# A long convolution with soft mixture-of-experts slots: spectra and z stored from all 128 partitions in one transfer, with row orders to match

## The chip, the cores and the metric

The kernel runs on one core of a Trainium2 chip. The metric is the device time of one execution in microseconds (us), as the median of several runs. The span is the part of the profiled execution between its first and its last instruction.

## The reference

```python
def _attn_ref(x, h):                      # x (8, 5696, 128), h (5696, 128), float32
    L = 2 * S
    Yf = np.fft.rfft(x, n=L, axis=1) * np.fft.rfft(h, n=L, axis=0)[None]
    return np.fft.irfft(Yf, n=L, axis=1)[:, :S, :]

def _moe_ref(x, phi, w1, w2):             # x (45568, 128), 8 experts of 4 slots, F = 1024
    logits = x @ phi                      # (45568, 32)
    d = softmax(logits, over all tokens)  # with max subtracted
    slot_input = (d.T @ x).reshape(8, 4, 128)
    slot_out = [relu(slot_input[e] @ w1[e]) @ w2[e] for e in range(8)]
    c = softmax(logits, over slots)
    return c @ slot_out
```

The output of the convolution, flattened to 45568 rows, is the input of the second part.

## The kernel before

The convolution of length 5696 = 89 x 64 is a two-stage transform done with matmuls against tables. All data are float32. The work is one pass over nine sequences: h (g = 0), then the eight batches of x (g = 1 to 8). The order of everything is written out by hand as a list of words that `run` walks through (`low`, `high`, `fold`, `loadf`, `forward`, `backward`, `flush`, `loadz`, `loadr`, `product`, ...), each word calling one stage with a running number; the schedule is manual and every engine executes in that order.

- `load_x` (L183) loads eight columns of a sequence, near and mirrored ones, into `xc`, `fold` (L216) adds and subtracts them on POOL.
- `stage_a` (L229) is the first transform: matmuls at L240 into a PSUM bank, copied by ACT (L242) into a staging tile `fst`, and from there stored to DRAM. The 64 low rows of the spectrum go to `fl`, the high rows of two chunks together to `fh`. Even and odd partitions of `fst` hold the two halves of the mirrored columns.
- `load_g` (L262, issue at L273) loads a group of up to four spectrum rows as `gt`, with the 128 positions in the partitions. `stage_b1` multiplies by `wt` (L286, into `bt`), and for g > 0 DVE multiplies by the transform of h (L305, L312); `stage_b2` transforms back with `vt` (L327, into `bz`) and ACT copies the result into the one staging tile `zst` (L332). After each second group, rows of `z` are stored: `zm` for the first 64, `zr` for the other 26.
- `load_main` (L375) and `load_rest` (L386) load eight columns of all rows as `zc` and `zx`. `stage_c1` does the last transform: L413 with `zc` and the table `im`, then L418 with `zx` and `ir` into the same banks. The later stages (L431 to L564) turn, compute the logits, both softmaxes and the dispatch. After the last batch come the experts and the output.

Stores are not issued where they are made: they are put on the list `pending` as closures, and a word `flush` issues all of them from SP (their line in the profile is L224, in `flush`). SP issues all loads too, in the order of the words, and it waits in that order. In the program SP's transfers take eight completion semaphores in turn, so a transfer waits for the one eight places before it.

The stores of one staging tile are made in a loop over its halves, each from 64 partitions with a step of two:

```python
for a in range(2):
    dst = fh[g][a, j // 2] if high else fl[g][a, j]
    pending.append(partial(
        nc.sync.dma_start, out=dst.rearrange("n r x -> r n x"),
        in_=st[a::2, :, :, :].rearrange("r n c d -> r n (c d)")))
```

In DRAM `fl` has the dimensions half, chunk j, column n, row, so that the half is the slowest, and a load reads 128 rows that lie 32 KB apart (16 KB in `fh`). `zm` has (parity o, row, column), `zr` has (parity, part c, row, column). The tables `wq`, `im`, `ir` are permuted on the host to the order in which positions land in the partitions.

Of the kernel before, what the change touches and what calls it, by code (L numbers as in the profile page):

```python
# [19 lines left out]
def transform_tables(S, N1, N2, CH, LOW, MAIN):  # L20

    N, R1, HALF, P = N1 * N2, S // N2, N2 // 2, 2 * N2  # L30
    k1 = np.arange(N1)
    alpha = np.pi * (k1 + 0.5) / N1
    m1 = np.arange(R1) - (N1 - 1) / 2
    a1 = np.outer(m1, alpha)
    part = np.stack([np.cos(a1), -np.sin(a1), -np.cos(a1)], 1)
    s1 = np.zeros((P, 3, N2 + HALF))
    for p, r in ((slice(0, P, 2), slice(0, N2)), (slice(P - 4 * (R1 - N2) + 1, P, 4), slice(N2, R1))):
        s1[p, :, 0:LOW] = part[r, :, 0:LOW]
        s1[p, :, N2:N2 + N1 - LOW] = part[r, :, LOW:]
    a0 = np.outer(alpha, np.arange(N1 // 2) + 0.5)  # L40
    part = np.stack([np.cos(a0), -np.sin(a0), -np.cos(a0)], 1)
    NP = N1 // 2
    im = np.zeros((2, MAIN, 2, N2))
    ir = np.zeros((2, 2, HALF, N2))
    for o in range(2):
        for c in range(2):
            im[o, :, c, 0:NP] = part[0:MAIN, o + c]
            ir[o, c, 0:N1 - MAIN, 0:NP] = part[MAIN:, o + c]
    k2 = np.arange(N2)
    omega = np.pi * (k1[:, None] + 2 * N1 * k2[None] + 0.5) / N  # L50
    m2 = np.arange(HALF) - (N2 - 1) / 2
    a2 = m2[None, :, None] * omega[:, None, :]
    w = np.concatenate([np.cos(a2), np.sin(a2)], 1)
    back = np.arange(N2).reshape(2, HALF).T.reshape(-1)
    NU = (NP + 1) // 2
    turn = (N1 - 1) / 2 * alpha[:, None] + (N2 - 1) / 2 * omega
    wq = np.zeros((2, N2, NP, N2))
    vq = np.zeros((2, N2, NU, 2, N2))
    tn = np.zeros((2, N2, 2, (NU + 1) // 2, 2, 2))
    rows = np.arange(N2).reshape(2, HALF // CH, CH)  # L60
    near = rows.transpose(1, 2, 0).reshape(-1)
    far = rows.reshape(2, -1, 2, CH).transpose(1, 3, 2, 0).reshape(-1)
    for a in range(2):
        wq[a] = w[a::2].transpose(1, 0, 2)
        wq[a] = np.concatenate([wq[a][near, 0:LOW // 2], wq[a][far, LOW // 2:]], 1)
        for q in range(NP):
            vq[q % 2, :, q // 2, a] = w[2 * q + a][back].T
            tn[q % 2, :, 0, q // 4, a, q // 2 % 2] = np.cos(turn[2 * q + a]) / N
            tn[q % 2, :, 1, q // 4, a, q // 2 % 2] = np.sin(turn[2 * q + a]) / N
    im, ir, wq, vq, tn = [t.reshape(P, *t.shape[k:]) for t, k in  # L70
                          ((im, 2), (ir, 3), (wq, 2), (vq, 2), (tn, 2))]
    return [np.ascontiguousarray(t, dtype=np.float32) for t in (s1, im, ir, wq, vq, tn)]
# [3 lines left out]
def kernel(  # L76
# [47 lines left out]
        nc.inline_tensor(t, f"tab_{n}").ap()  # L124
        for n, t in zip(("s1", "im", "ir", "w", "v", "turn"),
                        transform_tables(S, N1, N2, CH, LOW, MAIN))]
    fl = [nc.dram_tensor(f"fl_{g}", (2, NJ, CH, 2 * LOW // 2, 2 * D), F32, kind="Internal").ap()
          for g in range(B + 1)]
    fh = [nc.dram_tensor(f"fh_{g}", (2, NJ // 2, CH, 2 * HALF, 2 * D), F32, kind="Internal").ap()
          for g in range(B + 1)]  # L130
    zm = [nc.dram_tensor(f"zm_{b}", (2, MAIN, HALF, 2, D), F32, kind="Internal").ap() for b in range(B)]
    zr = [nc.dram_tensor(f"zr_{b}", (2, 2, HALF, HALF, D), F32, kind="Internal").ap() for b in range(2)]
    cd = nc.dram_tensor("c_t", (P, B * NQ, Q, 2, MH), F32, kind="Internal").ap()

    const = ctx.enter_context(tc.tile_pool(name="const", bufs=1))
# [93 lines left out]
    def stage_a(c, high):  # L229

        g, j = divmod(c, NJ)
        st = apool.tile([P, CH, 2, D], F32, name="fst", tag="fst", bufs=4)
        if high:
            groups = [(c_, o, HALF, slice(HP, HP + HALF)) for c_ in (c - 1, c) for o in range(2)]
        else:
            groups = [(c, o, HALF, slice(r, r + HALF)) for o in range(2) for r in (0, HALF)]
        for q in range(2):
            p = bank()
            for i, (c_, o, m, cols) in enumerate(groups):
                nc.tensor.matmul(p[i * m:(i + 1) * m, :], s1[:, q + o, cols], columns(c_, o),  # L240
                                 start=True, stop=True)
            nc.scalar.activation(st[:, :, q, :],  # L242
                                 p[:, :].rearrange("p (n d) -> p n d", d=D), AF.Copy)
        for a in range(2):
            dst = fh[g][a, j // 2] if high else fl[g][a, j]
            pending.append(partial(
                nc.sync.dma_start, out=dst.rearrange("n r x -> r n x"),
                in_=st[a::2, :, :, :].rearrange("r n c d -> r n (c d)")))
        if high:
            for c_ in (c - 1, c):  # L250
                del folded[c_]
# [10 lines left out]
    def load_g(u):  # L262
        if u >= (B + 1) * NW:
            return
        g, w, us = parts(u)
        n = sum(k for _, k in us)
        t_ = bpool.tile([P, 4, 2, D], F32, name="gt", tag="gt", bufs=3)
        if 8 * w < LOW:
            src = fl[g].rearrange("a j n (o k) x -> (a j n o) (k x)", o=2)
        else:  # L270
            src = fh[g].rearrange("a j n (o k) x -> (a j n o) (k x)", o=4)
        k0 = 4 * w % (LOW // 2) * 2 * D
        nc.sync.dma_start(  # L273
            out=t_[:, 0:n, :, :].rearrange("p q c d -> p (q c d)"), in_=src[:, k0:k0 + n * 2 * D])
        gs[u] = t_

    def stage_b1(u):
# [38 lines left out]
    def stage_b2(u):  # L316
        g, w, us = parts(u)
        if g == 0:
            return
        m = len(us)  # L320
        y_ = prods.pop(u)
        bz = bps.tile([P, 2, 2, 2 * D], F32, name="bz", tag=("bt", "bz")[u % 2])
        for o, (i, n) in enumerate(us):
            for q in range(n):
                r = slice(q * HP, (q + 1) * HP)
                for a in range(2):
                    nc.tensor.matmul(bz[a * HP:(a + 1) * HP, q, o, :], vt[r, i, a, :],  # L327
                                     y_[r, a * m + o, :, :].rearrange("p c d -> p (c d)"),
                                     start=True, stop=True)
        n = us[0][1]  # L330
        e_ = w % 4
        nc.scalar.activation(zst[:, e_, 0:m, 0:n, :].rearrange("p o q x -> p q o x"),  # L332
                             bz[:, 0:n, 0:m, :], AF.Copy)
        if w % 2 == 0:
            return
        k = 4 * e_ + m * n
        sv = zst[:, :, :, :, :].rearrange("p u o q x -> p (u o q) x")
        q0 = 4 * e_ - 4
        k0 = 8 * (w - 1)
        for o in range(2):  # L340
            if k0 < MAIN:
                pending.append(partial(
                    nc.sync.dma_start,
                    out=zm[g - 1][o, k0:k0 + 16].rearrange("(q a) r c d -> (a r) q (c d)", a=2),
                    in_=sv[o::2, q0:k, :]))
                continue
            for c in range(2):
                pending.append(partial(
                    nc.sync.dma_start,
                    out=zr[g % 2][o, c, k0 - MAIN:k0 - MAIN + 2 * (k - q0)].rearrange("(q a) r d -> (a r) q d", a=2),  # L350
                    in_=sv[o::2, q0:k, c * D:(c + 1) * D]))

    zs, ys, Ls, ds = {}, {}, {}, {}
# [13 lines left out]
    def load_main(T):  # L367
        if T >= NT:
# [5 lines left out]
        n = 2 * CH  # L374
        nc.sync.dma_start(  # L375
            out=t_[0][:, :, :, :, :].rearrange("p h n c d -> p (h n c d)"),
            in_=zm[b].rearrange("o k r c d -> (o k) r (c d)")[:, j * n:(j + 1) * n].rearrange(
                "p r x -> p (r x)"))

    def load_rest(T):  # L380
        if T >= NT:
# [3 lines left out]
        n = 2 * CH  # L385
        nc.sync.dma_start(  # L386
            out=t_[1][:, :, :, :].rearrange("p h n d -> p (h n d)"),
            in_=zr[(b + 1) % 2].rearrange("o c k r d -> (o c k) r d")[:, j * n:(j + 1) * n].rearrange(
                "p r x -> p (r x)"))

    def load_pair(T):
        load_main(T)
# [2 lines left out]
    def stage_c1(T, between=lambda: None):  # L395
# [18 lines left out]
                                     zt[r, h_, :, c, :], start=True, stop=False)  # L414
        for h_ in range(2):
            for (o, c), p in ps.items():
                r = slice((2 * o + c) * HALF, (2 * o + c) * HALF + N1 - MAIN)
                nc.tensor.matmul(p[h_ * HP:(h_ + 1) * HP, :], ir[r, :], zx[r, h_, :, :],  # L418
                                 start=False, stop=True)
        ps = {k: p[:, :].rearrange("p (n d) -> p n d", d=D) for k, p in ps.items()}  # L420
# [196 lines left out]
    nc.scalar.dma_start(out=ir[:, :], in_=t_ir)  # L617
    for i in range(8):
        nc.scalar.dma_start(
            out=zr[i // 4][i // 2 % 2, i % 2, N1 - MAIN:].rearrange("k (j r) d -> (k j) (r d)", r=2 * CH),  # L620
            in_=zring[0][1][0:4 * (HALF - N1 + MAIN), :, :, :].rearrange("p h n d -> p (h n d)"))
    held = {}

# [304 lines left out]
```

## Time and profile before

| | |
|---|---|
| median of 3 runs | 813.05 us (812.43 to 819.96) |
| profiled execution, its own time | 815.48 us |
| its span | 813.7 us |
| mean granted TensorE clock | 0.949 |
| busy | PE 717.6 us (88%), DVE 629.5 (77%), ACT 429.3 (53%), POOL 411.5 (51%) |
| moved by DMA | 282.51 MB, 347 GB/s over the span |
| stores to `fl`, `fh` | 144 and 72 transfers of 256 KB |
| stores to `zm` | 64 of 512 KB |
| stores to `zr` | 32 of 256 KB and 32 of 160 KB |
| loads `gt`, `zc`, `zx` | 108 of mostly 512 KB, 32 of 1024 KB (two into the tile `zd`), 32 of 512 KB (two into `zy`) |

In the profile PE is TensorE, DVE is VectorE, ACT is ScalarE, POOL is GpSimd, SP is SyncE. A name with q (SPq) is the sequencer that issues transfers. L224 is line 224 of the kernel. `fl<-fst` is a transfer or instruction that writes `fl` and reads `fst`. A busy PE is not PE at its peak, since matmuls are pipelined and their ends are modelled.

### The profile page before, as it was taken

Reading aid. Unit: us, or ns where it says so; the run is one execution under the profiler, and the core shown is the slowest. Engines: PE = TensorE matmul, PEld = TensorE weight load, DVE = VectorE, ACT = ScalarE, POOL = GpSimd, SP = SyncE. Lnnn points to the kernel's source line nnn. Section 1 sums busy time; section 2 is a strip of 40 time slices with the busy share of each in tenths; the row PEclk is TensorE's granted clock in tenths of the full one; section 3 lists DMA queues with packets and bytes.
Section 4 is the critical chain, followed back from the end, with each engine's and each line's share of the span. In section 5 each row is a group of like instructions: output and inputs, shape, how many; then the busy total and the mean of one; then the engine's idle time right before and its main releaser. Section 6 shows DMA issues by size and latency. Waiting matters only on the chain.

```text
span 813.7 us, 22006 instructions
## 1 busy us (share of the span) xinstructions
PE 717.6 (88%) x8884; PEld 367.0 (45%) x8884; DVE 629.5 (77%) x895; ACT 429.3 (53%) x868; POOL 411.5 (51%) x368
## 2 busy tenths in 40 slices
PE   5767888869999999999999999999998887888893
PEld 1322233324544444444444455554444443356882
DVE  1029987638988998798999899988998997795642
ACT  2323345326666665566666666665664545474532
POOL 5655434224566666466656666655533443587000
PEclk9989999879999999999999999999999999999755
DMA  8999999999999999999999999999999898873998
GB/s 293 359 329 384 328 393 386 323 348 344 367 355 364 395 372 328 369 355 382 353 387 381 384 349 390 379 352 366 341 321 343 301 354 288 318 267 106 378 401 353
DMA packets 167661, 282.51 MB, mean 347 GB/s; under 512 B 11305, under 2 KB 130729, under 8 KB 162345
## 3 DMA queue, kind: packets, MB, share of 16 engines
q1 hardware_dynamic: 166552, 280.02, 96.6%
q8 instruction: 70, 1.15, 0.5%
q10 hardware_dynamic: 1008, 1.10, 0.4%
q14 instruction: 31, 0.25, 0.1%
HBM read 148.54 MB, written 132.53 MB: 345 GB/s over the span
## 4 chain that ended last, share of the span: by engine, by line
PE 55%; DMA 18%; DVE 15%; ACT 4%; POOL 2%; issue 2%; SPq 1%; ACTq 0%; DVEq 0%; POOLq 0%
PE bank L240 17%; PE bt L286 8%; PE bz L327 7%; PE bank L413 6%; DMA out_dram<-o 5%; PE bank L418 4%; DMA zx<-zr 4%; DVE yf L305 4%; DVE bt L305 4%; PE bank L441 3%; DMA xc<-in_h_dram 3%; PE bank L450 2%; DVE yf L312 2%; PE bank L540 2%; PE bank L564 2%
## 5 line engine op out<-in xcount | busy, mean ns | idle before, releaser
L240 PE MATMUL bank<-x,s 128*32 128x512 f32 x1728 | 209.1, 607 | 14.1 <-POOL x L216 8.3
L216 POOL TENSOR_TENSOR x<-xc 128x512 f32<-128x512 f32 x144 | 179.2, 1278 | 81.4 <-PE bank L240 55.5
L242 ACT ACTIVATE fst<-bank 128x512 f32<-128x512 f32 x216 | 125.8, 595 | 87.1 <-PE bank L240 50.7
L286 PE MATMUL bt<-gt,wt 64*64 64x256 f32 x1620 | 117.1, 398 | 27.4 <-DMA gt<-fl 9.4
L332 ACT ACTIVATE zst<-bz 128x1024 f32<-128x1024 f32 x96 | 93.0, 968 | 82.8 <-PE bz L327 72.5
L431 POOL TENSOR_TENSOR y<-y,op 128x512 f32<-128x512 f32 x64 | 78.4, 1225 | 112.8 <-DVE op L405 110.3
L305 DVE TENSOR_TENSOR yf<-bt,Hi 128x1024 f32<-128x1024 f32 x96 | 112.5, 1172 | 17.9 <-PE bt L286 17.8
L312 DVE TENSOR_TENSOR yf<-bt,yf 128x512 f32<-128x512 f32 x192 | 119.3, 663 | 3.3
L240 PEld LDWEIGHTS bank<-x,s 128*32 128x32 f32 x1728 | 56.1, 111 | 130.4 <-issue 90.8
L305 DVE TENSOR_TENSOR bt<-bt,Hr 128x1024 f32<-128x1024 f32 x96 | 113.0, 1177 | 0.0
L327 PE MATMUL bz<-yf,vt 64*64 64x256 f32 x1440 | 101.4, 390 | 4.8 <-DVE yf L312 4.4
L286 PEld LDWEIGHTS bt<-gt,wt 64*64 64x64 f32 x1620 | 54.7, 135 | 89.0 <-issue 28.8
L527 POOL TENSOR_TENSOR L<-L,rs 128x512 f32<-128x512 f32 x32 | 33.7, 1052 | 108.1 <-DVE rs L522 57.2
L327 PEld LDWEIGHTS bz<-yf,vt 64*64 64x64 f32 x1440 | 55.0, 137 | 41.1 <-DVE yf L312 12.9
L431 POOL TENSOR_TENSOR y<-y,om 128x512 f32<-128x512 f32 x54 | 64.3, 1190 | 2.1
L421 ACT ACTIVATE y<-bank 128x512 f32<-128x512 f32 x32 | 19.1, 597 | 87.4 <-PE bank L418 87.4
L441 PE MATMUL bank<-ident,y 109*128 109x109 f32 x512 | 59.2, 261 | 3.7 <-POOL y L431 1.7
L413 PE MATMUL bank<-zc,im 64*64 64x512 f32 x480 | 60.6, 599 | 0.1
L441 PEld LDWEIGHTS bank<-ident,y 109*128 109x128 f32 x512 | 49.7, 141 | 13.3 <-issue 7.4
L443 ACT ACTIVATE yt<-bank 128x360 f32<-128x360 f32 x128 | 52.6, 476 | 4.1 <-PE bank L441 3.9
L305 DVE TENSOR_TENSOR yf<-bt,turn 128x1024 f32<-128x1024 f32 (+1 forms) x12 | 14.1, 1171 | 52.3 <-PE bt L286 52.3
L405 DVE TENSOR_TENSOR y<-bank,y 128x512 f32<-128x512 f32 x32 | 22.1, 691 | 39.7 <-ACT y L421 36.4
(99 smaller groups left out, 881.7 us busy)
## 6 DMA issues: line engine op xcount, KB each, us to landing
fl<-fst SPq DMA_DIRECT2D x144, 256.0 KB, 6.4
gt<-fl SPq DMA_DIRECT2D x72, 512.0 KB, 8.3
zm<-zst SPq DMA_DIRECT2D x64, 512.0 KB, 6.9
zc<-zm SPq DMA_DIRECT2D x30, 1024.0 KB, 8.1
fh<-fst SPq DMA_DIRECT2D x72, 256.0 KB, 7.2
xc<-in_x_dram SPq DMA_DIRECT2D x32, 512.0 KB
out_dram<-o SPq DMA_DIRECT2D x16, 1024.0 KB, 5.2
zx<-zr SPq DMA_DIRECT2D x30, 512.0 KB
```

The costliest lines, as they stand in the source:

```text
L216: nc.gpsimd.tensor_tensor(out=y_[:, o, :, :], in0=near, in1=far, op=AL.subtract if o else AL.add)
L240: nc.tensor.matmul(p[i * m:(i + 1) * m, :], s1[:, q + o, cols], columns(c_, o), start=True, stop=True)
L242: nc.scalar.activation(st[:, :, q, :], p[:, :].rearrange("p (n d) -> p n d", d=D), AF.Copy)
L286: nc.tensor.matmul(bt[q * HP:(q + 1) * HP, a, o, :], wt[r, 2 * i + q, :], t_[r, 2 * o + q, :, :].rearrange("p c d -> p (c d)"), start=True ...
L305: nc.vector.tensor_tensor(out=p_, in0=pv, in1=h_, op=AL.mult)
L312: nc.vector.tensor_tensor(out=y_[r, 0:k, c, :], in0=pv[:, :, c, :], in1=y_[r, 0:k, c, :], op=op_)
L327: nc.tensor.matmul(bz[a * HP:(a + 1) * HP, q, o, :], vt[r, i, a, :], y_[r, a * m + o, :, :].rearrange("p c d -> p (c d)"), start=True, sto ...
L332: nc.scalar.activation(zst[:, e_, 0:m, 0:n, :].rearrange("p o q x -> p q o x"), bz[:, 0:n, 0:m, :], AF.Copy)
L413: nc.tensor.matmul(ps[o, c][h_ * HP:(h_ + 1) * HP, :], im[r, c, :], zt[r, h_, :, c, :], start=True, stop=False)
L431: eng.tensor_tensor(out=part_, in0=part(v, 0), in1=o_[:, :, :], op=sign)
L441: nc.tensor.transpose(p[:, i * TR:(i + 1) * TR], ys[T][0:TR, k * CH + i, 0:D], ident[0:TR, 0:TR])
L443: nc.scalar.activation(yt[:, k * CH:(k + 1) * CH, :, :], of_tokens(p), AF.Copy)
```

## The change

The two halves of a store become one transfer from all 128 partitions. For this the DRAM tensors get their dimensions in another order: the half (or the parity o) moves inside the chunk, so that rows of both halves lie where one access pattern reaches them. The loads then read with two dimensions in DRAM, of which the outermost has 16, 32 or 64 entries. The order of the 128 positions in `gt`, `zc` and `zx` changes with that, and the tables are permuted on the host to match. `zr`'s 160 KB stores (five rows) stay one for each parity and part. The matmul with `zx` uses all 32 rows of a block instead of 26; the six others hold zeros.

```diff
@@ transform_tables
+    rest = np.zeros((HALF, *part.shape[1:]))
+    rest[0:N1 - MAIN] = part[MAIN:]
+    main, rest = [t.reshape(-1, 8, 2, *t.shape[1:]).transpose(1, 2, 0, 3, 4).reshape(t.shape)
+                  for t in (part[0:MAIN], rest)]
...
-            im[o, :, c, 0:NP] = part[0:MAIN, o + c]
-            ir[o, c, 0:N1 - MAIN, 0:NP] = part[MAIN:, o + c]
+            im[o, :, c, 0:NP] = main[:, o + c]
+            ir[c, o, :, 0:NP] = rest[:, o + c]
...
-    near = rows.transpose(1, 2, 0).reshape(-1)
-    far = rows.reshape(2, -1, 2, CH).transpose(1, 3, 2, 0).reshape(-1)
+    near = rows.transpose(2, 0, 1).reshape(-1)
+    far = rows.reshape(2, -1, 2, CH).transpose(3, 2, 0, 1).reshape(-1)
@@ DRAM tensors
-    fl: (2, NJ, CH, 2 * LOW // 2, 2 * D)
+    fl: (NJ, 2, CH, 2, LOW // 2, 2 * D)
-    fh: (2, NJ // 2, CH, 2 * HALF, 2 * D)
+    fh: (NJ // 2, 2, CH, 2, 2, HALF // 2, 2 * D)
-    zm: (2, MAIN, HALF, 2, D)
+    zm: (MAIN // 16, 2, 8, 2, HALF, 2, D)
-    zr: (2, 2, HALF, HALF, D)
+    zr: (HALF // 16, 2, 2, 8, 2, HALF, D)
@@ stage_a
-        for a in range(2):
-            dst = fh[g][a, j // 2] if high else fl[g][a, j]
-            pending.append(partial(
-                nc.sync.dma_start, out=dst.rearrange("n r x -> r n x"),
-                in_=st[a::2, :, :, :].rearrange("r n c d -> r n (c d)")))
+        if high:
+            dst = fh[g][j // 2].rearrange("a n c o k x -> (c o k) (a n) x")
+        else:
+            dst = fl[g][j].rearrange("a n o k x -> (o k) (a n) x")
+        pending.append(partial(
+            nc.sync.dma_start, out=dst, in_=st[:, :, :, :].rearrange("r n c d -> r n (c d)")))
@@ load_g
-            src = fl[g].rearrange("a j n (o k) x -> (a j n o) (k x)", o=2)
+            src = fl[g].rearrange("j a n o k x -> (a n o) j (k x)")
...
-            src = fh[g].rearrange("a j n (o k) x -> (a j n o) (k x)", o=4)
+            src = fh[g].rearrange("j a n c o k x -> (a n c o) j (k x)")
@@ stage_b2
+        if k0 < MAIN:
+            pending.append(partial(
+                nc.sync.dma_start,
+                out=zm[g - 1][k0 // 16].rearrange("o q a r c d -> (a r) (o q) (c d)"),
+                in_=sv[:, q0:k, :]))
+            return
+        for c in range(2):
+            dst = zr[g % 2][(k0 - MAIN) // 16, c, :, 0:k - q0]
+            if k - q0 == 8:
+                pending.append(partial(
+                    nc.sync.dma_start, out=dst.rearrange("o q a r d -> (a r) (o q) d"),
+                    in_=sv[:, q0:k, c * D:(c + 1) * D]))
                 continue
-            for c in range(2):
+            for o in range(2):
                 pending.append(partial(
                     nc.sync.dma_start, out=dst[o].rearrange("q a r d -> (a r) q d"),
                     in_=sv[o::2, q0:k, c * D:(c + 1) * D]))
@@ load_main, load_rest
-            in_=zm[b].rearrange("o k r c d -> (o k) r (c d)")[:, j * n:(j + 1) * n]...
+            in_=zm[b][:, :, :, :, j * n:(j + 1) * n].rearrange("u o q a r c d -> (o q a) u (r c d)"))
-            in_=zr[(b + 1) % 2].rearrange("o c k r d -> (o c k) r d")[:, j * n:(j + 1) * n]...
+            in_=zr[(b + 1) % 2][:, :, :, :, :, j * n:(j + 1) * n].rearrange("u c o q a r d -> (c o q a) u (r d)"))
@@ stage_c1
-                r = slice((2 * o + c) * HALF, (2 * o + c) * HALF + N1 - MAIN)
+                r = slice((2 * c + o) * HALF, (2 * c + o + 1) * HALF)
```

More of the change, by code (lines that the diff above doesn't have):

```diff
@@ L126 @@
                         transform_tables(S, N1, N2, CH, LOW, MAIN))]
-    fl = [nc.dram_tensor(f"fl_{g}", (2, NJ, CH, 2 * LOW // 2, 2 * D), F32, kind="Internal").ap()
+    fl = [nc.dram_tensor(f"fl_{g}", (NJ, 2, CH, 2, LOW // 2, 2 * D), F32, kind="Internal").ap()
           for g in range(B + 1)]
-    fh = [nc.dram_tensor(f"fh_{g}", (2, NJ // 2, CH, 2 * HALF, 2 * D), F32, kind="Internal").ap()
+    fh = [nc.dram_tensor(f"fh_{g}", (NJ // 2, 2, CH, 2, 2, HALF // 2, 2 * D), F32, kind="Internal").ap()
           for g in range(B + 1)]
-    zm = [nc.dram_tensor(f"zm_{b}", (2, MAIN, HALF, 2, D), F32, kind="Internal").ap() for b in range(B)]
-    zr = [nc.dram_tensor(f"zr_{b}", (2, 2, HALF, HALF, D), F32, kind="Internal").ap() for b in range(2)]
+    zm = [nc.dram_tensor(f"zm_{b}", (MAIN // 16, 2, 8, 2, HALF, 2, D), F32, kind="Internal").ap() for b in range(B)]
+    zr = [nc.dram_tensor(f"zr_{b}", (HALF // 16, 2, 2, 8, 2, HALF, D), F32, kind="Internal").ap() for b in range(2)]
     cd = nc.dram_tensor("c_t", (P, B * NQ, Q, 2, MH), F32, kind="Internal").ap()
@@ L268, in load_g @@
         if 8 * w < LOW:
-            src = fl[g].rearrange("a j n (o k) x -> (a j n o) (k x)", o=2)
+            src = fl[g].rearrange("j a n o k x -> (a n o) j (k x)")
         else:
-            src = fh[g].rearrange("a j n (o k) x -> (a j n o) (k x)", o=4)
+            src = fh[g].rearrange("j a n c o k x -> (a n c o) j (k x)")
         k0 = 4 * w % (LOW // 2) * 2 * D
         nc.sync.dma_start(
-            out=t_[:, 0:n, :, :].rearrange("p q c d -> p (q c d)"), in_=src[:, k0:k0 + n * 2 * D])
+            out=t_[:, 0:n, :, :].rearrange("p q c d -> p (q c d)"), in_=src[:, :, k0:k0 + n * 2 * D])
         gs[u] = t_
@@ L339, in stage_b2 @@
         k0 = 8 * (w - 1)
-        for o in range(2):
-            if k0 < MAIN:
+        if k0 < MAIN:
[7 more added lines that the diff above has]
+            if k - q0 == 8:
                 pending.append(partial(
-                    nc.sync.dma_start,
-                    out=zm[g - 1][o, k0:k0 + 16].rearrange("(q a) r c d -> (a r) q (c d)", a=2),
-                    in_=sv[o::2, q0:k, :]))
+                    nc.sync.dma_start, out=dst.rearrange("o q a r d -> (a r) (o q) d"),
+                    in_=sv[:, q0:k, c * D:(c + 1) * D]))
                 continue
-            for c in range(2):
+            for o in range(2):
                 pending.append(partial(
-                    nc.sync.dma_start,
-                    out=zr[g % 2][o, c, k0 - MAIN:k0 - MAIN + 2 * (k - q0)].rearrange("(q a) r d -> (a r) q d", a=2),
+                    nc.sync.dma_start, out=dst[o].rearrange("q a r d -> (a r) q d"),
                     in_=sv[o::2, q0:k, c * D:(c + 1) * D]))
@@ L376, in load_main @@
             out=t_[0][:, :, :, :, :].rearrange("p h n c d -> p (h n c d)"),
-            in_=zm[b].rearrange("o k r c d -> (o k) r (c d)")[:, j * n:(j + 1) * n].rearrange(
-                "p r x -> p (r x)"))
+            in_=zm[b][:, :, :, :, j * n:(j + 1) * n].rearrange("u o q a r c d -> (o q a) u (r c d)"))
     def load_rest(T):
@@ L387, in load_rest @@
             out=t_[1][:, :, :, :].rearrange("p h n d -> p (h n d)"),
-            in_=zr[(b + 1) % 2].rearrange("o c k r d -> (o c k) r d")[:, j * n:(j + 1) * n].rearrange(
-                "p r x -> p (r x)"))
+            in_=zr[(b + 1) % 2][:, :, :, :, :, j * n:(j + 1) * n].rearrange("u c o q a r d -> (c o q a) u (r d)"))
     def load_pair(T):
@@ L619 @@
         nc.scalar.dma_start(
-            out=zr[i // 4][i // 2 % 2, i % 2, N1 - MAIN:].rearrange("k (j r) d -> (k j) (r d)", r=2 * CH),
+            out=zr[i // 4][1, i // 2 % 2, i % 2, (N1 - MAIN) // 2 - 8:].rearrange(
+                "q a (j r) d -> (q a j) (r d)", r=2 * CH),
             in_=zring[0][1][0:4 * (HALF - N1 + MAIN), :, :, :].rearrange("p h n d -> p (h n d)"))
```

## The prediction

> **What bounds the kernel now.** I read the page's busy slices and its lines on the DMA queues first, then windows of one batch period each, then the waits for `zx`, then SP's timeline ahead of one such wait, and last the packet records.
>
> ```profile
> PE   5767888869999999999999999999998887888893
> DMA  8999999999999999999999999999999898873998
> ...
> DMA packets 167661, 282.51 MB, mean 347 GB/s; under 512 B 11305, under 2 KB 130729, under 8 KB 162345
> ...
> q1 hardware_dynamic: 166552, 280.02, 96.6%
> ```
>
> From the third slice to the 33rd PE is close to full, and the DMA engines are full too (9 is 90% or more). The packets on SP's own queue alone fill 96.6% of 16 engines' span. Two resources are level, so I looked at whole batches. The product of a batch's first tile starts near 213.7, 290.0, 370.2, 445.7 and 521.1 us in the chain of waits:
>
> ```profile
> 213.70:290.00 76.30, 75.14 (x957) 37.39 (x960) 69.31 (x97) 47.85 (x97) 47.04 (x40) 1.00 1.04 369
> 290.00:370.00 80.00, 76.89 (x952) 38.45 (x952) 69.11 (x97) 47.74 (x97) 47.07 (x40) 0.98 1.01 355
> 370.00:445.60 75.60, 75.12 (x958) 37.38 (x956) 69.39 (x97) 47.90 (x97) 47.05 (x40) 1.00 1.05 376
> 445.60:521.00 75.40, 74.92 (x953) 37.32 (x952) 69.19 (x97) 47.71 (x97) 47.05 (x40) 1.00 1.04 375
> 521.00:600.00 79.00, 75.68 (x954) 37.08 (x956) 70.22 (x100) 48.05 (x99) 44.12 (x38) 1.00 1.02 353
> ```
>
> The columns are the stretch, its length, then busy time of PE, PEld, DVE, ACT, POOL, then clock, DMA share, GB/s. The third and fourth period last 75.4 to 75.6 us, and PE is busy for all but 0.5 us: PE sets that pace. The first lasts 76.3, the second 80, the last 79. In the second, PE does 76.9 us of work with its clock at 0.98, and the bytes flow at 355 GB/s in place of 376. The DMA share can exceed 1 because two packets overlap on an engine. It stands at 1.04 to 1.05 where no one waits and is at most 1.06 in 20 us windows elsewhere (100 to 120 us), so the DMA engines have about 1% to spare per period, some 0.7 us. What PE waits for where it waits:
>
> ```profile
> PEld bank L418 <- DMA zx<-zr: 17.8, 7, 7.6
> ...
> PE bank L418 <- DMA zx<-zr: 11.7, 4, 6.7
> ```
>
> The 17.8 and 11.7 us are what PE's two halves lose to the load of `zx`; it is the one large wait of PE for a transfer. SP's timeline ahead of the one at 325 us:
>
> ```profile
> 303.39 5.52 SPq L224 DMA_DIRECT2D zr<-zst  x4
> 309.01 2.02 SPq L224 DMA_DIRECT2D fl<-fst  x2
> 311.15 3.75 SPq L224 DMA_DIRECT2D zr<-zst  x4
> 315.32 0.33 SPq L273 DMA_DIRECT2D gt<-fl  x1
> 315.70 0.44 SPq L375 DMA_DIRECT2D zc<-zm  x1
> 316.24 1.33 SPq L199 DMA_DIRECT2D xc<-in_x_dram  x2
> 317.67 0.53 SPq L575 DMA_DIRECT2D c_t<-cst  x1
> 318.31 0.37 SPq L386 DMA_DIRECT2D zx<-zr  x1
> ```
>
> SP issues eight `zr` stores and two `fl` stores in 11.5 us, then a `gt` load (315.32), `zc` (315.70), `xc` (316.24) and the small `c_t` (317.67), and at 318.31 the `zx` load for which PE waits. Its issue takes 0.37 us and its landing 7 us more, since 2.4 MB stand ahead of it. In the packet records the DMA engines run without a gap from 300 to 325 us. This wait is DMA capacity, not SP's speed.
>
> **The change part by part.** All stores of `fl`, `fh` and `zm` and the 256 KB stores of `zr` go in pairs, one from the even and one from the odd partitions, at one flush. Each pair becomes one transfer of the same bytes in packets of the same size (1 KB; 512 B for `zr`). Transfers removed: 72 of `fl`, 36 of `fh`, 32 of `zm`, 16 of `zr`, together 156 of some 700, 18 in each batch. The 32 `zr` stores of 160 KB stay. No compute instruction is added, removed or moved. The matmul at L418 reads 32 rows of `zx` instead of 26, same columns; its time (638 ns median) goes with its 512 columns, cost nothing, a bound of 32/26 of its weight load (131 ns) being hidden under matmuls.
>
> *DMA engine time of the stores.* In the packet records a 1 KB packet lasts 46 ns, a completion packet 9 ns. Where two `fl` stores of 256 KB stand queued, the second's packets start 0.74 us after the first's (74 pairs, median); two `zm` stores of 512 KB start 1.44 us apart (30 pairs). One boundary is thus worth 2 x 0.74 - 1.44 = 0.04 us. 156 x 0.04 = 6.2 us over the span, 0.7 us a batch. Bounds: the completion packets alone, 156 x 9 ns = 1.4 us, and 18 us if a boundary cost what a straight-line fit of packets against time gives a completion (0.117 us). I take 6.2, measured directly.
>
> *SP's time.* Stores cost SP 0.58 us at least, whatever their size; the 128-row loads 0.32:
>
> ```profile
> L224 SPq DMA_DIRECT2D fl<-fst x144: 579/630/2048, 14.8 to 601.8; - x144
> ...
> L224 SPq DMA_DIRECT2D zm<-zst x64: 579/679/3681, 107.1 to 665.6; - x64
> ```
>
> ```profile
> L273 SPq DMA_DIRECT2D gt<-fl x72: 319/432/1676, 47.9 to 636.3; - x72
> ```
>
> (Columns: min/median/max ns, first and last start.) 18 stores less save 18 x (0.58 + 0.04 to the next) = 11 us of SP in a batch. But the 20 loads of a batch (12 `gt`, 4 `zc`, 4 `zx`) now have an outermost DRAM dimension of 16, 32 or 64 instead of 128. The nearest rows are the `xc` loads with 64 rows (0.54 to 0.64 us) and the last output store with 16 rows of 8 (0.74). So a load costs 0.22 to 0.42 us more, 4 to 8 us a batch; I take 0.26, the 64-row row, 5 us. SP gains about 6 us a batch. SP waits on its own for buffers (60.6 us at L273 for PE's `bt`), so almost none of this is on the path. It would count where the DMA queue runs empty: near 48 us, where the first `gt` load waits for the last store, and in the tail after 673 us, where SP issues eight `zr` stores at 0.66 us each; there six issues remain, but the four loads behind them cost 0.3 us more each, which cancels it.
>
> *Waits.* SP's transfers take eight completion semaphores in turn, so a transfer is issued only once the eighth before it has landed. About 6 are outstanding on average with 2.4 MB in steady state. Fewer, larger transfers loosen this. The order in the queue is the same, so no load has more bytes ahead of it than before; no wait is added. A half-store could land earlier than the pair, but every reader waits for both halves.
>
> *The loads' addresses.* [...] Packets of 4 KB last 159 ns by median, in the mean 186 for `gt` from `fl`, 169 from `fh`, 205 for `zx`; 8 KB of `zc` 309 and 338. Over 16 engines these loads are 107 + 37 + 52 + 87 = 283 us. If all ran at the fastest, 36 us would go; if all were stretched as `zx` is (205/159), 34 us would come. I take nothing, the middle: the mean follows neither the step (`zx` and `gt` from `fh` have the same 16 KB) nor the size.
>
> [...] No row here shows a loss that grows with the step.
>
> **The sum.** The boundaries count only where the DMA engines set the pace. The head to 48 us holds 12 merges, 0.5 us. From 48 to 213.7 DVE and PE take turns, and the DMA-bound piece near 150 to 170 us holds some ten merges: 0.5. The first two full periods exceed 75.4 us by 0.9 and 4.8; with 0.7 us more slack a batch, which doubles what there is, I let 60% of the 5.7 go (an estimate): 3.5. The period from 521 exceeds by 3.6, partly since its work thins out: 1.5. The tail: 0.5. In the steady periods PE hides the gain; were PE not there, 0.7 each would show. Sum 6.5 us: the span goes from 813.7 to 807.2, the profiled execution from its own 815.48 to 809. The median of the runs shown is 813.05, 2.4 below the profiled one, so I forecast 806.5. About 1%, 8 us, is what a measurement of this kernel can tell from no change.
>
> **The rivals.**
> - *The reads turn slow (slower).* Place: `gt`, `zc`, `zx`. For it: the loads hold over a third of the DMA time and there is 1% of slack. [...] It decides once the loads cost more than the slack and the gain, 1.4 us a batch or 12 us in all (4%). At the upper end of 34 us, 4 us a batch, 2.6 x 8.5 batches = 22 us show: 835. At three quarters of it, 828.
> - *All stalls go (faster).* Added slack ends every wait for `zx`: 5.7 + 3.6 from the periods, half of the 9 us that PE loses in the window 150 to 175, 0.5 in the head, 2 of SP's time in the tail: 16 us, 797. For it: the two clean periods show that a batch behind by 3 us less waits for nothing. Against: the wait at 165 us starts with a full queue.
> - *PE hides everything (no change).* The stalls come from DMA that is behind by 7 us (two `zx` waits of 3 us and the slow clock), and 0.2 us of merges ahead of each `zx` load is too little: 812.
> - *It does not do what it says.* The transfers would be split again in descriptors; the packets are of the same size either way, so this is the 812 again.
>
> **Chances.** Forecast 0.32, its own range 802 to 810; the bound of 1% (805) cuts through that range, so 0.12 of it counts as faster by over 1% and 0.20 as no change. All stalls go 0.26. PE hides everything and not-what-it-says 0.22. Slow reads 0.20, nearly all over 1%. Faster 0.38, within 1% 0.42, slower 0.20. The range takes in the faster rival's 797 and three quarters of the slow reads, 828.
>
> **What would show it.** Right: stores of 512 KB and 1 MB in the list of issues, 156 fewer completion packets on each engine, SP's stores still near 0.6 us, all loads' packets within a few per cent, the periods at 75.4, the waits for `zx` well under 29.5 us. Wrong: periods equal but longer than 76 with PE idle and a DMA share at 1.05 (slow reads); periods unchanged with the same `zx` waits (PE or a full queue); a total under 800 (boundaries cost more than 0.04).

## The result and the profile after

The changed kernel takes 855.86 us (median of 6 runs, 855.81 to 860.07) where the kernel before, run beside it, takes 814.07: ratio 1.051, 95% interval 1.047 to 1.055. It is 42 us slower. The profiled execution took 855.86 us, its span is 854.1.

The page of the changed kernel, as before: busy slices, packets, SP's own DMA queue.

```profile
PE   5867787779988998999799979998999787888892
DMA  8999999999999999999999999999999988774998
...
DMA packets 165162, 282.49 MB, mean 331 GB/s; under 512 B 8808, under 2 KB 128232, under 8 KB 159848
...
q1 hardware_dynamic: 164056, 280.01, 97.7%
```

The bytes are the same 282.5 MB, and there are 2499 packets fewer, nearly all under 512 B: the 156 x 16 completion packets of the merged transfers. But packets of SP's queue take 97.7% of a span of 854.1 us, that is 834 us, where they took 96.6% of 813.7, that is 786 us. The same data cost the DMA engines 48 us more. The list of issues (KB each, median us to landing) shows the merged stores:

```profile
fl<-fst SPq DMA_DIRECT2D x72, 512.0 KB, 9.6
gt<-fl SPq DMA_DIRECT2D x72, 512.0 KB, 10.0
zm<-zst SPq DMA_DIRECT2D x32, 1024.0 KB, 11.7
```

`gt` from `fl` now lands 10.0 us after its issue; before, the list had 8.3:

```profile
gt<-fl SPq DMA_DIRECT2D x72, 512.0 KB, 8.3
```

Four periods, taken from the matmuls of L421 at 214.5, 298.8, 382.6, 464.9 and 547.3 us in the chain of waits (stretch, length, busy time of PE, PEld, DVE, ACT, POOL, clock, DMA share, GB/s):

```profile
214.50:298.80 84.30, 77.89 (x960) 37.86 (x960) 69.56 (x97) 47.86 (x96) 47.24 (x41) 0.96 1.04 344
298.80:382.60 83.80, 78.81 (x956) 38.50 (x960) 69.16 (x97) 47.81 (x96) 47.02 (x41) 0.94 1.05 342
382.60:464.90 82.30, 76.56 (x956) 38.08 (x960) 69.16 (x97) 47.77 (x96) 47.01 (x41) 0.98 1.05 340
464.90:547.30 82.40, 76.56 (x956) 37.91 (x959) 69.17 (x97) 47.76 (x96) 47.03 (x41) 0.98 1.05 343
```

PE was busy for all but 0.5 us of a 75.5 us period; now it is idle for 5 to 6.4 us of 82 to 84. The share of the DMA engines stands at its ceiling of 1.04 to 1.05 while the rate is 340 to 344 GB/s in place of 369 to 376: the engines are full and slow. PE's own work also takes longer, 76.6 to 78.8 us a period for some 75.1, at a granted clock of 0.94 to 0.98 for 1.00; no run here separates that part from the waits. PE's waits for transfers, after:

```profile
PEld bank L426 <- DMA zx<-zr: 28.6, 7, 6.2
PE bt L291 <- DMA gt<-fl: 24.8, 13, 6.9
PE bank L426 <- DMA zx<-zr: 21.7, 7, 5.4
PEld bt L291 <- DMA gt<-fl: 17.0, 8, 7.8
```

And before, for `gt` from `fl`:

```profile
PE bt L286 <- DMA gt<-fl: 9.4, 3, 6.5
PEld bt L286 <- DMA gt<-fl: 7.4, 1, 7.4
```

The waits for `zx` grew from 17.8 and 11.7 us, and PE's two halves now wait 41.8 us for `gt` from `fl`, 16.8 before.

The cleanest place to see the cause is the head, where the first three `gt` loads follow each other with nothing else in flight. The windows view inside that stretch, of the kernel before and then of the changed one; the last column is GB/s:

```profile
49.50:53.00 3.50, 1.30 (x12) 0.80 (x16) 0.00 (x0) 0.00 (x0) 0.49 (x1) 0.50 0.99 384
```

```profile
48.00:54.00 6.00, 3.09 (x24) 1.19 (x28) 1.04 (x1) 0.00 (x0) 0.23 (x1) 0.50 1.00 247
```

Inside these windows the loads of 512 KB flow at 384 GB/s before and at 247 after, with the DMA share at 0.99 and 1.00. The windows leave out the first load's start and, before, the end of the last; from the first packet of the three loads to their last landing it is 5.2 us before and 7.0 after. In the packet records a 4 KB packet of `gt` from `fl` lasts 262 ns in the mean and 265 by median, where it lasted 186 and 159. The others moved less, and both ways: `gt` from `fh` 169 to 183, `xc` 170 to 187, `zx` 205 to 185, `zc` (8 KB) 338 to 331, the 1 KB packets of the `fl` and `zm` stores 46.7 to 46.8. The excess of `gt` from `fl` is 72 x 128 packets x 76 ns / 16 engines = 44 us, the size of the loss.

### The profile page after: what moved, and what is told of

Read it like the earlier page. It is cut to its first block, busy times and chain, and to the rows that moved or that the text cites. A ratio compares the mean times of both kernels' runs of the same rounds, so it can differ in the third digit from the quotient of the medians.

```text
span 854.1 us, 21789 instructions
## 1 busy us (share of the span) xinstructions
PE 729.3 (85%) x8884; PEld 369.8 (43%) x8884; DVE 628.2 (74%) x895; ACT 429.4 (50%) x868; POOL 410.9 (48%) x368
## 2 busy tenths in 40 slices
DMA packets 165162, 282.49 MB, mean 331 GB/s; under 512 B 8808, under 2 KB 128232, under 8 KB 159848
## 3 DMA queue, kind: packets, MB, share of 16 engines
q1 hardware_dynamic: 164056, 280.01, 97.7%
## 4 chain that ended last, share of the span: by engine, by line
PE 47%; DMA 32%; DVE 7%; ACT 4%; SPq 3%; POOL 3%; issue 2%; ACTq 0%; DVEq 0%; POOLq 0%
PE bank L244 14%; PE bt L291 8%; DMA zx<-zr 8%; DMA gt<-fl 7%; PE bz L332 6%; DMA out_dram<-o 5%; DMA fl<-fst 4%; PE bank L421 4%; PE bank L426 4%; DMA zr<-zst 3%; PE bank L449 3%; POOL y L439 2%; PE bank L548 2%; DMA xc<-in_h_dram 2%; DMA cl<-c_t 1%
## 5 line engine op out<-in xcount | busy, mean ns | idle before, releaser
L244 PE MATMUL bank<-x,s 128*32 128x512 f32 x1728 | 209.4, 607 | 11.7 <-POOL x L220 8.8
L291 PE MATMUL bt<-gt,wt 64*64 64x256 f32 x1620 | 122.0, 412 | 37.6 <-DMA gt<-fl 24.8
L244 PEld LDWEIGHTS bank<-x,s 128*32 128x32 f32 x1728 | 53.3, 111 | 131.3 <-issue 91.8
L291 PEld LDWEIGHTS bt<-gt,wt 64*64 64x64 f32 x1620 | 57.3, 139 | 103.3 <-issue 36.9
L332 PEld LDWEIGHTS bz<-yf,vt 64*64 64x64 f32 x1440 | 56.8, 140 | 40.9 <-DVE yf L317 10.8
L421 PE MATMUL bank<-zc,im 64*64 64x512 f32 x480 | 61.9, 609 | 10.9 <-DMA zc<-zm 10.9
L426 PE MATMUL bank<-zx,ir 32*64 32x512 f32 x480 | 37.6, 685 | 21.7 <-DMA zx<-zr 21.7
## 6 DMA issues: line engine op xcount, KB each, us to landing
zm<-zst SPq DMA_DIRECT2D x32, 1024.0 KB, 11.7
```

What stands on the lines that cost most here:

```text
L291: nc.tensor.matmul(bt[q * HP:(q + 1) * HP, a, o, :], wt[r, 2 * i + q, :], t_[r, 2 * o + q, :, :].rearrange("p c d -> p (c d)"), start=True ...
L421: nc.tensor.matmul(ps[o, c][h_ * HP:(h_ + 1) * HP, :], im[r, c, :], zt[r, h_, :, c, :], start=True, stop=False)
```

## The experiments

The first four ask what makes that load slow: the number 16 in its outermost DRAM dimension (it is the only load with 16; `gt` from `fh` and `zc` have 32, `zx` 64), or the 512 KB between the rows of its inner dimension.

**Sixteen rows of eight, with the old addresses and the old stores.** On the kernel before, a gap of 4 KB after each 256 KB of `fl`, so that the load can't be written with one dimension; its inner rows stay 32 KB apart:

```diff
-    fl_{g}: (2, NJ, CH, 2 * LOW // 2, 2 * D)
+    fl_{g}: (2 * NJ, CH * LOW + 4, 2 * D), the last 4 rows of each block unused
-            src = fl[g].rearrange("a j n (o k) x -> (a j n o) (k x)", o=2)
+            src = fl[g].rearrange("a j n (o k) x -> (a j) (n o) (k x)", o=2)
```

> [...] Stores in halves as before. Theory division (an outermost dimension of 16 is what slows the load, whatever the addresses): gt packets of 4 KB near 262 ns in the mean as in the changed kernel, time 840 to 856 us. Theory step (rows 512 KB apart slow it): gt packets near 186 ns, time 811 to 818 us.

855.57 us, ratio 1.051 (1.046 to 1.056); `gt` packets 259 ns. The windows line of the three loads, and the queue's line of the page:

```profile
49.00:55.00 6.00, 3.11 (x24) 1.19 (x28) 1.06 (x1) 0.00 (x0) 0.33 (x1) 0.51 1.03 253
```

```profile
q1 hardware_dynamic: 166552, 280.02, 97.4%
```

With stores in halves and neighbouring rows 32 KB apart, the way in which the load is divided makes all of the loss by itself: 253 GB/s. The theory of the step falls.

**The changed kernel with one dimension of 128 rows in the load.**

```diff
-    fl_{g}: (NJ, 2, CH, 2, LOW // 2, 2 * D)
+    fl_{g}: (2, CH, NJ, 2, LOW // 2, 2 * D)
-            src = fl[g].rearrange("j a n o k x -> (a n o) j (k x)")
+            src = fl[g].rearrange("a n j o k x -> (a n j o) (k x)")
-    near = rows.transpose(2, 0, 1).reshape(-1)
+    near = rows.transpose(2, 1, 0).reshape(-1)
```

> The changed kernel with fl in the order half, column, chunk, so that the gt load from fl reads 128 rows 32 KB apart with one dimension, as before the change, and the merged store writes 64 KB pieces 512 KB apart. All other merged stores and loads as changed. If the gt load from fl is the whole loss, under either theory: gt packets near 186 ns, time 803 to 815 us. If the merged stores cost something themselves: over 820 us.

812.56 us, ratio 0.997 (0.993 to 1.001), `gt` packets 179 ns, and in the three loads:

```profile
49.00:53.00 4.00, 1.76 (x16) 0.80 (x16) 0.00 (x0) 0.00 (x0) 1.01 (x1) 0.64 0.97 378
```

The loss is gone with this one load, so the other changed loads and the merged stores carry none of it. Runs of this kernel spread widely (805 to 817 us); it can't be told from the kernel before.

**The changed kernel with the step off its power of two**, 4 KB between the chunks of `fl`, so that the inner rows of the load are 516 KB apart and not 512; the outermost dimension stays 16:

```diff
-    fl_{g}: (NJ, 2, CH, 2, LOW // 2, 2 * D)
+    fl_{g}: (NJ, 2 * CH * 2 * (LOW // 2) + 4, 2 * D), the last 4 rows of each chunk unused
```

> [...] Theory step: the loss goes or is halved, gt packets under 210 ns, time 805 to 830 us. Theory division: no difference, packets near 262 ns, 852 to 858 us.

849.13 us (1.037 to 1.053 of before); packets 254 ns instead of 262.

```profile
49.50:55.00 5.50, 2.73 (x20) 1.00 (x24) 0.68 (x1) 0.00 (x0) 0.39 (x1) 0.53 1.02 257
```

Nearly no difference, as the theory of division has it. The fall of some 7 us lies outside what it named (852 to 858), and is a sixth of the loss; it is not clear of noise, since the changed kernel's ratio to before (1.047 to 1.055) overlaps this one's.

**The changed kernel with 32 outermost rows.** Two chunks stand side by side:

```diff
-    fl_{g}: (NJ, 2, CH, 2, LOW // 2, 2 * D)
+    fl_{g}: (NJ // 2, 2, CH, 2, 2, LOW // 2, 2 * D)
-            dst = fl[g][j].rearrange("a n o k x -> (o k) (a n) x")
+            dst = fl[g][j // 2, :, :, j % 2].rearrange("a n o k x -> (o k) (a n) x")
-            src = fl[g].rearrange("j a n o k x -> (a n o) j (k x)")
+            src = fl[g].rearrange("j a n i o k x -> (a n i o) j (k x)")
```

with the table's rows in the order (column, i, o, j).

> The changed kernel with two chunks side by side in fl, so that the gt load from fl has 32 outermost rows 32 KB apart and 4 steps of 1 MB. Theory division (16 is special, 32 is not, as the zc load with 32 x 4 keeps 331 ns for 8 KB): gt packets 170 to 200 ns, time 803 to 818 us. Theory step (1 MB is no better than 512 KB): packets 225 ns or more, time over 835 us.

805.59 us, packets 179 ns. The three loads, the queue, and three periods:

```profile
51.00:55.00 4.00, 2.17 (x20) 0.99 (x24) 0.12 (x1) 0.00 (x0) 0.00 (x0) 0.50 1.00 369
```

```profile
q1 hardware_dynamic: 164056, 280.01, 96.2%
```

```profile
283.60:359.00 75.40, 74.78 (x960) 37.13 (x960) 69.22 (x97) 47.76 (x96) 47.11 (x41) 1.00 1.04 380
359.00:433.90 74.90, 74.72 (x956) 37.07 (x958) 69.21 (x97) 47.75 (x96) 47.06 (x41) 1.00 1.05 378
433.90:509.90 76.00, 74.79 (x957) 37.13 (x960) 69.25 (x97) 47.76 (x96) 47.11 (x41) 1.00 1.03 373
```

Doubling the outermost dimension from 16 to 32 takes 50 us off. The inner rows are then 1 MB apart, twice the step of the slow load. The periods are at 75 to 76 us with PE busy for all but 0.2 to 1.2 us: PE sets the pace again.

**What is wrong with 16?** Two theories were left: the number itself, or the partitions, of which each of the 16 outermost rows fills eight neighbouring ones. Which engine writes them is not shown, since no packet record names an engine. On the kernel before I cut each `gt` load from `fl` in two transfers with 64 outermost rows, once to partitions 0 to 63 and 64 to 127, once to the even and the odd ones:

```diff
+        halves = [slice(i * HP, (i + 1) * HP) for i in range(2)]    # first run
+        halves = [slice(i, P, 2) for i in range(2)]                 # second run
+        for r in halves:
             nc.sync.dma_start(
-                out=t_[:, 0:n, :, :]..., in_=src[:, k0:k0 + n * 2 * D])
+                out=t_[r, 0:n, :, :]..., in_=src[r, k0:k0 + n * 2 * D])
```

> The kernel before, with each gt load from fl as two transfers, to partitions 0 to 63 and 64 to 127, from 64 neighbouring rows each. [...] Theory count (the number 16 of outermost rows is slow in itself, whatever the partitions): 64 outermost rows are fine, packets 165 to 195 ns, time 810 to 825 us, the 72 more transfers included.

> The kernel before, with each gt load from fl as two transfers, to the even and to the odd partitions, from every second row. The control of the run with halves 0 to 63 and 64 to 127: the same number of transfers, bytes and packets, but each transfer reaches all groups of partitions. [...]

Contiguous halves: 864.6 us (one run), packets 261 ns, median 267. Even and odd: 837.6 us (one run), packets 179 ns, median 159. The head of the two, in the same order:

```profile
47.50:53.00 5.50, 3.86 (x20) 1.26 (x24) 0.72 (x1) 0.00 (x0) 0.92 (x1) 0.55 1.04 244
```

```profile
50.50:54.50 4.00, 1.84 (x16) 0.90 (x16) 0.00 (x0) 0.00 (x0) 0.44 (x1) 0.50 0.90 304
```

The same number of transfers, of packets and of outermost rows; the packets of the one look like those of the 16-row load (261 and 262 ns), those of the other like the kernel's before. So a number of 16 isn't needed for slow packets. The partitions differ, and with them the DRAM rows of one transfer: 64 neighbours 32 KB apart, or every second row, 64 KB apart. No run varies the DRAM rows alone; against them speaks that `gt` from `fh` reads all its rows from 2 MB with packets of 169 ns. That the partitions are what slows the load is thus the likelier reading, not a proof.

The second run missed the time expected of fast packets, 837.6 us for 810 to 825. Its packets are fast (179 ns), but the DMA share in the head is 0.90: the engines idle a tenth of the time between transfers of 256 KB. The last of the six lands late, and from the first packet of the three loads to their last landing it is 6.8 us, as long as with contiguous halves (6.9). So the reading rests on the packets' times, not on the rates of the two windows. Over the whole run the packets of SP's queue take 9.5 us more than before, and the engines idle 12.6 us more. I come back to that below.

**What merging is worth.** The 32-row kernel measured again, and beside it the same kernel with all stores in halves, layouts and loads kept:

```diff
-        pending.append(partial(nc.sync.dma_start, out=dst, in_=st[:, :, :, :]...))
+        for a in range(2):
+            pending.append(partial(nc.sync.dma_start, out=dst[a], in_=st[a::2, :, :, :]...))
```

> The changed kernel with 32 outermost rows in the gt load from fl, once more with more rounds: 803 to 808 us, ratio to before 0.987 to 0.993.

> The same with every store of fl, fh, zm and zr in two halves again (even and odd partitions) and all layouts and loads kept. Theory of the prediction: merging is worth 0.04 us of DMA time a boundary, 156 boundaries, so 3 to 7 us more than the merged kernel: 809 to 813 us. Rival (merging is worth nothing, the gain over before comes from the row orders of the loads): equal within 1 us.

806.28 us, ratio 0.992 (0.988 to 0.995), against 814.62, ratio 1.001 (0.997 to 1.004). Merging 156 pairs saves 8.3 us, somewhat more than the 3 to 7 expected; the new row orders save nothing of their own. The 32-row kernel is 0.8% faster than the kernel before (0.5 to 1.2%).

**Are stores from contiguous halves slow too?** The last kernel with the `fl` and `fh` stores in halves 0 to 63 and 64 to 127 instead of even and odd:

> The 32-row kernel with the fl and fh stores in halves, from partitions 0 to 63 and 64 to 127 instead of the even and the odd ones; number of transfers and bytes as in the run with stores in halves (814.6 us). [...]

850.7 us, ratio 1.047 (1.040 to 1.054). Packets: `fl` 49.8 ns (46.7), `fh` 47.1 (46.4). The queue's lines, with even and odd halves and then with contiguous ones:

```profile
q1 hardware_dynamic: 166552, 280.02, 95.9%
```

```profile
q1 hardware_dynamic: 166552, 280.02, 94.9%
```

Expected were packets of 65 ns or more with a time over 850 us, or packets of 46 to 48 ns with 808 to 820 us. Neither held as a whole: the time is that of the first, the packets are near those of the second. The time is 36 us longer. In the two profiled executions the spans are 816.0 and 847.7 us; 95.9% and 94.9% of them are 783 and 804 us, so 21 us more packet time, 7 of it in `fl`, 6 in `zc` and the rest spread, and 10 us more idle. PE's two halves wait 44 us for `gt` from `fl`, 20 with even and odd halves. Stores in these contiguous halves are bad too, though not by much longer packets; by what is open. Their DRAM side changes as well: a half writes 32 rows of eight pieces instead of 64 of four, and no run separates that from the partitions.

**The price of more transfers.** The 32-row kernel with merged stores and its `gt` loads from `fl` cut in even and odd partitions:

> The 32-row kernel with merged stores and each gt load from fl in two transfers, to even and odd partitions: 72 transfers more, still 84 fewer than before. On the kernel before the same split cost 24 us, far more than 72 boundaries of 0.04 us. If that came from the eight completion semaphores (too many transfers for eight places), the smaller count here gives 805 to 815 us. If each further load costs 0.33 us by itself, 826 us or more.

822.1 us (816 to 828; 1.008 to 1.020 of before), between the two expectations: 16 us for 72 more transfers, 0.22 each, where the same cut of the partitions on the kernel before cost 24 (one run). With 84 transfers fewer than before the loss is still there, so the completion semaphores are not the whole of it. Merging pairs of stores paid 8.3 / 156 = 0.05 us each. Why a cut load costs four times what a cut store costs is not settled; what speaks for SP's issue rate, without a run that varies it, is that a 64-row load takes SP about 0.6 us per 256 KB (six in 3.70 us in the head of the run with even and odd partitions; a 128-row load of 512 KB 0.32 at least). That is close to the 0.7 us that the engines need for it (256 KB at the 369 to 384 GB/s of whole fast loads in the head, an estimate), so that nothing builds up ahead of them.

## Why the prediction was wrong

- *What bounds the kernel.* Held. The DMA engines had about 1% to spare per period; 48 us of added packet time, 44 of them in `gt` from `fl`, came out as 40 us of span. One reading is off: of the 2.4 MB "ahead" of the `zx` load at 318.31 us, 1.8 MB were ahead and 0.5 its own.
- *The stores' DMA time.* Came out near. 0.04 us a boundary and 6.5 us in all were forecast; the kernels that differ in the merging alone differ by 8.3 us, 0.05 a boundary. That it is so near is in part luck: the 0.04 is a difference of two medians, and the starts of paired `fl` stores in that trace lie 0.68 to 1.70 us apart. The shortest gaps, 0.68 us and for `zm` 1.36, would have given nothing.
- *SP's time.* The loads with two dimensions in DRAM cost SP 0.51 us at least, 0.32 before; 0.26 more was taken, 0.2 is right. (min/median/max ns:)

```profile
L278 SPq DMA_DIRECT2D gt<-fl x72: 514/570/3974, 45.9 to 678.4; - x72
```

- *Waits.* "No load has more bytes ahead of it" is true and was no help: the bytes ahead moved more slowly.
- *The loads' addresses.* This is the step that failed. It priced the new order of the loads at nothing, with ends of -36 and +34 us. Measured, `gt` from `fl` alone added 44 us, beyond the upper end, while `zx` got faster. The upper end was made from `zx`, the slowest load of the trace. The trace before holds no load of 16 rows of eight, so no row could bound it. With the division undone (32 rows of four, 806 us) the loss is gone. The step looked at DRAM addresses alone; it did not ask how the load's 128 rows are divided, and which partitions an outermost row then fills.
- *The rival "the reads turn slow"* had the right sign and about half the size (22 us at its upper end, 42 measured), but of its three loads only `gt` slowed much, and it left open why. The step between rows is not the cause: old addresses, 32 KB apart, are slow with 16 rows of 8 (259 ns), and rows 1 MB apart are fast with 32 (179 ns).
- *Chances.* Slower had 0.20, and the range ended at 828.

What the runs show is that the division of this one load makes the loss. That it does so through the partitions is inferred from the load to contiguous halves: its packets last 261 ns, as those of the slow load (262), against 179 to even and odd partitions and 186 in whole loads of 128 rows. How is not shown: the packet records hold no engine, so no run tells which rows an engine reads or which partitions it writes.

## What to carry to other kernels

When a layout is changed so that a store can be merged, look at how the load on the other side is then divided: here a load written as 16 rows of 8 over the same bytes ran at 247 GB/s in the head and as 32 rows of 4 at 369. That all DMA engines are busy is not enough (a share of 1.00 in both cases); compare the rate of that one transfer in a stretch where nothing else runs, before trusting the sum. Merging pairs of stores in a DMA-bound kernel was worth 0.05 us a pair, some 1% here, once the loads were whole.

## What was not expected of the hardware

- A load to 64 contiguous partitions and one to 64 partitions two apart, of equal bytes and packets, have packets of 261 and 179 ns. Their DRAM rows differ as well, neighbours or every second one.
- The slow load ends in as many completion packets as the fast one: 8808 packets under 512 B are 2497 fewer than before, which the 156 removed stores account for with 16 each. How the engines shared the slow load is not shown.
- Cutting a load in two cost 0.2 to 0.3 us a piece with fast packets, four to six times what merging a pair of stores saved.
